# A fused state-space scan and MLP kernel: second x block behind two of five w1 chunks, row-paired matmuls for it, b1 columns from TensorE, first mm2 waiting by w2 chunk, a new order

## The chip, the cores and the metric

One core of a Trainium2 chip runs one launch. The metric is device time in microseconds (us). Every run gives one time; a profiled execution also gives a trace, from which come a page of summaries and answers to single questions. A span in the trace runs from the first to the last instruction and is shorter than the time of the run, which holds what lies around it.

Engines: PE is TensorE (matmuls; its weight loads, LDWEIGHTS, are listed as PEld), DVE is VectorE, ACT is ScalarE, POOL is GpSimd, SP is the sync engine, which here only issues DMAs.

## The reference

x is (1, 2048, 448) in bf16, and the same normalized x feeds two branches:

```
xn  = layernorm(x)
s   = scan(xn)          # complex diagonal state of 448, 2048 steps, plus xn * Dskip
y   = layernorm(xn)
h   = gelu(y @ w1 + b1) # w1: 448 x 1792
g   = silu(h @ w2 + b2) # w2: 1792 x 448
out = x + s * g
```

## The kernel before

**Tiling.** The 2048 rows are taken as 8 blocks of 256, and a block as 128 partitions with two rows each (par 0 and 1, even and odd rows). Four groups g of two blocks (b 0 and 1) pass through the same stages: layernorm statistics on DVE (`ln_stats`, `ln_scale`), application (`ln_apply`), transposition of the normalized rows (`xt`) into `xnT` (scan branch) and `xn2T` (MLP branch), `bu` (PE, L647, the scan's input product), `ssm` (DVE scans, L672), `mm1` (PE, L721, gelu on ACT, L731), `mm2` (PE, L755, bias on DVE L758, silu on ACT L759), and `ym` (PE, L785 to L791, product on DVE L794, addition L797, store).

**The first group is special.** Its MLP input does not come by DMA transposes but by PE: `first_norm` normalizes block 0 in two halves (par 0 and 1; DVE L393, L394, L398; ACT L395, L396), transposes each on PE (L401), copies it out of PSUM on DVE (L405), and five filler matmuls (L403) follow each. Block 1 then gets its statistics on DVE (L379, L383), its scale by ten small DVE instructions (`ln_scale`, L422 to L432), its application (L448), eight transposes on PE (L464) and one copy (L470). `mm1_half(j, b)` computes hidden columns 2j and 2j+1 (two of 14 pieces of 128) for one block: eight matmuls of 128 rows and 256 columns (L741) and one gelu on ACT (L747), seven j for b=0 and then seven for b=1. The bias enters as one more row of w1: `w1_sb[64, 3, :]` holds b1 and the moving operand holds a 1 there.

**mm1 of later groups** has 64-row matmuls. D = 448 is seven times 64, so hidden column 2j+k takes seven passes of 64 rows; passes of the upper and the lower half of the partitions alternate, so that two run at a time. The last 64 rows of w1 must then also lie in partitions 64 to 127: W0 to W3 copy them there (ACT L836 or DVE L837), over the b1 row. The bias comes from `b1f`, columns made from `b1b`, which four small DMAs (B0 to B3) load and POOL casts (BF, L356).

**Loads.** SP issues in order: x block 0 in two halves, x block 1, w1 in chunks (`CH`: 4, 4, 4 and 2 of the 14 pieces; each chunk two DMAs, rows 0 to 383 and the last 64 rows), the scan's B matrices (Bn0, Bn60, Bn1, Bn61), w2 in four chunks, b2, B0 to B3, x blocks 2 and 3, and then the transposing DMAs: two of `xnT` for g=0, seven of `BT` (from the LB results that DVE makes of B), then `xmT1` (`xn2T` of g=1), `Ct` (C matrices), `xnT1`, `xmT0` (`xn2T` of g=2).

**The order.** Every instruction is a numbered or tagged task. `ORDER` is one list of all tasks; an engine takes its own in that order, and waits are semaphores worked out from the keys that tasks read and write. `SECOND` names the tasks that take the second of two possible engines. A task waits once, before its first instruction, for all that it needs: mm2 for all four w2 chunks.

PE's sequence up to g=2 is, in words: 28 warm-up matmuls (L821), the parameter columns (L480 to L484), transposes and fillers of block 0, `mm1_half` j=0 to 4 of block 0, the eight transposes of block 1, j=5 and 6, the seven j of block 1, then mm2, mm2, bu, mm2, bu, mm2, bu (L755 and L647, from 20.01 us on), then mm1 of g=1 (H10 to H16) with two more bu between, and then mm1 of g=2, which begins with H21 at 49.88 us.

Of the kernel before, what the change touches and what calls it, by code (L numbers as in the profile page):

```python
# [7 lines left out]
ACT = mybir.ActivationFunctionType  # L8
ALU = mybir.AluOpType
# [8 lines left out]
class Task:  # L18
# [3 lines left out]
    __slots__ = ("eng", "ins", "reads", "writes", "sem", "idx", "deps", "chain", "alts", "tag")  # L22

    def __init__(self, eng, ins, reads, writes, sem):
# [3 lines left out]
        self.tag = None  # L28
        self.alts = [(eng, ins)]
# [7 lines left out]
class Plan:  # L37
# [55 lines left out]
    def link(self):  # L93
        last, readers = {}, {}
        for t in self.tasks:
            for k in t.reads:
                if k in last:
                    t.deps.add(last[k])
            for k in t.writes:
# [12 lines left out]
    def emit(self):  # L112
# [8 lines left out]
        for t in order:  # L121
# [3 lines left out]
            need = {}  # L125
            for d in t.deps:
                sem, val = done[d]
                if need.get(sem, 0) < val:
                    need[sem] = val
            for sem, val in need.items():  # L130
                if seen.get(sem, 0) < val:
                    eng.wait_ge(self.sems[sem], val)
                    seen[sem] = val
            for k, fn in enumerate(t.ins):
                last = fn(eng)
# [26 lines left out]
0 9 18 22 10 1 19 23 16 20 15 88 2 11 21 3 27 12 26 8 17 14 13 24 5 7 89 25 6 4 28 90 96 91 29 45 97 92 98 30 93 46 94 99 48 49 47 31 103 95  # L162
53 100 50 54 101 32 52 102 55 62 33 105 51 114 56 34 106 35 107 116 108 63 109 64 36 65 DH 37 118 104 38 115 57 39 117 120 66 58 110 119 40
111 122 148 121 41 146 142 143 112 42 123 124 B0 113 147 B1 126 155 60 125 B2 154 61 153 59 149 B3 72 152 128 69 67 44 156 127 68 70 150 151
130 129 160 73 167 132 158 131 168 169 134 159 133 157 136 184 171 135 170 161 138 172 185 173 140 139 175 174 275 43 141 W0 176 186 177 BF
71 137 82 305 74 W1 75 178 187 77 79 179 86 306 76 272 78 304 80 195 81 83 307 310 85 188 309 308 311 276 162 312 189 233 W2 163 281 313 234
316 287 314 322 180 315 317 235 284 W3 164 273 318 323 319 412 278 165 282 192 166 236 410 277 413 190 283 320 285 237 279 196 414 411 193
416 288 H10 238 417 415 280 418 324 181 H11 321 364 366 393 419 H12 422 516 365 183 239 518 368 517 367 191 242 H13 240 522 521 H14 241 182
# [26 lines left out]
def bass_recurrent_scan__ssm_conv_s5__mixer_channel_mlp__prompt_kernel(  # L195
# [18 lines left out]
    with ExitStack() as es:  # L214
# [75 lines left out]
        with nc.Block():  # L290
# [53 lines left out]
            for c in (1, 2, 3):  # L344
                ldw1(c, S1 + 3)
# [568 lines left out]
```

## Time and profile before

| what | value |
|---|---|
| time, median of 3 runs | 156.45 us (156.44 to 156.95) |
| time of the profiled execution | 156.73 us, its span 155.0 us |
| PE busy | 148.7 us, 96% of the span |
| DVE, ACT, POOL busy | 127.2, 108.2, 39.7 us |
| first mm1 matmul (L741) | at 6.74 us |
| first mm2 matmul (L755) | at 20.01 us |
| first mm1 matmul of g=1 (L721) | at 35.46 us |
| first mm1 matmul of g=2 (L721) | at 49.88 us |
| last PE matmul begins its group | at 151.84 us |

How to read the trace's rows: a timeline row gives start, duration, engine, line, operation, tiles and count, and in brackets how long the engine sat idle before it and what ended that. A matmul's duration in the trace holds its way through the array and overlaps the next matmul; the time that one more matmul costs (its pitch) is the difference of the starts. For example 72 matmuls of L741 from 12.15 to 20.01 us have a pitch of 109 ns, though each lasts 273 ns.

### The profile page before, as it was taken

What the parts mean: (1) busy time and instruction counts of PE and PEld (TensorE: products, weight loads), DVE (VectorE), ACT (ScalarE), POOL (GpSimd) and SP (SyncE); (2) the same over time, 40 slices, a digit from 0 to 9 for tenths busy, and PEclk for the clock granted to TensorE, in tenths of its full rate; (3) what the DMA queues carried; (4) which work ended last, traced back from release to release, by engine and by line L of the source; (5) the groups of instructions that cost most, each with busy time, mean ns of one, the idle gap of its engine ahead of it and who ended that gap; (6) DMA issues with size and microseconds to landing.
All of it is one profiled execution on the core that took longest, in us unless ns stands there. A gap on an engine that the chain in (4) does not pass through costs nothing.

```text
span 155.0 us, 3005 instructions
## 1 busy us (share of the span) xinstructions
PE 148.7 (96%) x1072; PEld 90.3 (58%) x1072; DVE 127.2 (82%) x276; ACT 108.2 (70%) x183; POOL 39.7 (26%) x117
## 2 busy tenths in 40 slices
PE   6889999999997999999999999999999999999992
PEld 6789956665553655555544447665666454555551
DVE  5898999989998999889999936369948559984974
ACT  3769899984997799979989793640592893393200
POOL 6575072000036633000049330000471700000021
PEclk9999999999999999999999999999999999999999
DMA  4999999898997003000005340005030000100013
GB/s 118 297 286 353 284 154 185 209 197 195 211 109 153 0 0 68 4 2 0 0 4 127 59 118 0 4 20 98 4 118 0 2 0 0 66 0 0 0 59 118
DMA packets 31512, 14.04 MB, mean 91 GB/s; under 512 B 25733, under 2 KB 31113, under 8 KB 31498
## 3 DMA queue, kind: packets, MB, share of 16 engines
q1 hardware_dynamic: 31344, 13.80, 40.6%
q8 instruction: 8, 0.13, 0.4%
q10 hardware_dynamic: 154, 0.06, 0.1%
q14 instruction: 6, 0.05, 0.1%
HBM read 6.20 MB, written 1.84 MB: 52 GB/s over the span
## 4 chain that ended last, share of the span: by engine, by line
PE 68%; DVE 14%; ACT 7%; DMA 6%; issue 3%; SPq 2%; ACTq 0%; DVEq 0%
PE psum L755 21%; PE psum L721 14%; PE psum L785 13%; PE psum L647 9%; PE psum L788 4%; PE psum L636 4%; DMA w_sb<-in_B_w_dram 3%; DMA xn2T<-xn_sb 2%; ACT WT L579 2%; DVE Bn L598 2%; SPq L90 2%; PE psum L741 2%; DVE lnst L379 2%; DVE xn_sb L448 1%; ACT xn_sb L449 1%
## 5 line engine op out<-in xcount | busy, mean ns | idle before, releaser
L755 PE MATMUL psum<-w_sb,gT 128*128 128x448 bf16 x224 | 44.2, 353 | 0.0
L721 PE MATMUL psum<-xn2T,w_sb 64*128 64x512 bf16 x294 | 33.6, 378 | 1.0 <-DMA xn2T<-xn_sb 0.9
L755 PEld LDWEIGHTS psum<-w_sb,gT 128*128 128x128 bf16 x224 | 21.8, 98 | 19.4 <-issue 0.2
L731 ACT ACTIVATE gT<-psum,b1f 128x512 bf16<-128x512 f32 x42 | 25.7, 687 | 5.2 <-PE psum L721 5.1
L721 PEld LDWEIGHTS psum<-xn2T,w_sb 64*128 64x128 bf16 x294 | 15.9, 109 | 17.1 <-issue 3.0
L647 PE MATMUL psum<-xnT,BT 128*128 128x256 bf16 x196 | 24.0, 273 | 0.0
L647 PEld LDWEIGHTS psum<-xnT,BT 128*128 128x128 bf16 x196 | 18.9, 98 | 5.3 <-issue 0.8
L794 DVE TENSOR_TENSOR t<-psum,g_sb 128x448 bf16<-128x448 f32 (+2 forms) x17 | 10.0, 592 | 9.7 <-PE psum L788 8.8
L759 ACT ACTIVATE g_sb<-o 128x448 bf16<-128x448 f32 x16 | 9.1, 573 | 8.2 <-DVE o L758 8.2
L672 DVE TENSOR_TENSOR_SCAN s_f<-cw,cur,v_sb 128x256 f32<-128x256 f32 x21 | 14.6, 737 | 0.2
L741 PE MATMUL psum<-xn2T,w_sb 128*128 128x256 bf16 x112 | 12.7, 273 | 0.8 <-DVE xn2T L405 0.4
L741 PEld LDWEIGHTS psum<-xn2T,w_sb 128*128 128x128 bf16 x112 | 11.8, 111 | 1.4 <-DMA w_sb<-in_B_w_dram 0.7
L769 POOL TENSOR_TENSOR xr<-xd,g_sb 128x448 f32<-128x448 bf16 x4 | 4.4, 1090 | 31.3 <-ACT g_sb L759 24.3
L758 DVE TENSOR_TENSOR o<-psum,b2bc 128x448 f32<-128x448 f32 x16 | 9.8, 613 | 2.9 <-PE psum L755 2.4
L785 PE MATMUL psum<-CZ,h_sb 128*128 128x448 bf16 x56 | 11.9, 353 | 0.0
L448 DVE TENSOR_SCALAR xn_sb<-x_all,lnw 128x448 bf16<-128x448 bf16 (+1 forms) x31 | 10.8, 382 | 0.9 <-DMA xn2T<-xn_sb 0.7
L651 ACT ACTIVATE u_sb<-psum 128x512 bf16<-128x512 f32 x12 | 7.0, 587 | 5.4 <-PE psum L647 5.4
L785 PE MATMUL psum<-CQ,h_sb 128*128 128x448 bf16 (+2 forms) x54 | 10.5, 332 | 0.0
L747 ACT ACTIVATE gT<-psum 128x512 bf16<-128x512 f32 x14 | 8.3, 595 | 3.1 <-PE psum L741 2.9
L595 ACT ACTIVATE tmp<-Cr,cw 128x448 f32<-128x448 bf16 (+1 forms) x12 | 8.0, 665 | 1.3 <-DVE CQ L598 0.6
L785 PEld LDWEIGHTS psum<-CZ,h_sb 128*128 128x128 bf16 x56 | 5.2, 98 | 5.9 <-issue 0.8
L379 DVE BATCH_NORM_STATS2 lnst<-x_all 128x6 f32<-128x448 bf16 x14 | 8.1, 615 | 0.1
(156 smaller groups left out, 217.4 us busy)
## 6 DMA issues: line engine op xcount, KB each, us to landing
out_dram<-tmp SPq DMA_DIRECT2D x7, 224.0 KB, 1.9
w_sb<-in_B_w_dram SPq DMA_DIRECT2D x3, 448.0 KB, 7.5
x_all<-in_A_x_dram SPq DMA_DIRECT2D x3, 448.0 KB, 4.8
w_sb<-in_B_w_dram SPq DMA_DIRECT2D x3, 384.0 KB, 5.4
Bn<-in_A_B_re_dram SPq DMA_DIRECT2D x1, 336.0 KB, 5.5
Bn<-in_A_B_im_dram SPq DMA_DIRECT2D x1, 336.0 KB, 5.7
x_all<-in_A_x_dram SPq DMA_DIRECT2D x2, 112.0 KB, 2.1
x_all<-in_A_x_dram SPq DMA_DIRECT2D x1, 224.0 KB, 2.8
```

The source lines that it names most:

```text
L379: dve([lambda e, b=b, par=par, q=q: e.bn_stats(lnst[:, q, :], x_all[:, 2 * g + b, par, :])], [f"x{2 * g + b}"] + (["xmT0p1"] if (g, b) == ...
L448: on = [("dve", [lambda e, o=o, i=i: e.tensor_scalar(o, i, rs, nb, op0=ALU.mult, op1=ALU.add) for o, i in pairs], 0.4, 0.12), ("act", [lam ...
L647: fns = [lambda e, r=r, m=m, d=d: e.matmul(psum[:, 4, r * NK:(r + 1) * NK], BT[:, m, d, :], xnT[:, gx, d, :], start=(d == 0), stop=(d == 6 ...
L672: dve(lambda e, i=i, ri=ri, init=init: e.tensor_tensor_scan(s_f[:, i, ri, :], col(R2, i).to_broadcast([128, NK]), v_sb[:, i, ri, :], init, ...
L721: return lambda e: e.matmul(psum[:, b0 + k, :], w1_sb[halves[h], d, fcol(2 * j + k)], rhs[halves[h], d, :, :], start=first and d == 0, sto ...
L731: act([lambda e, k=k: e.activation(gT[:, gb, 2 * j + k, :], psum[:, b0 + k, :], ACT.Gelu_apprx_tanh, bias=b1f[:, 2 * j + k:2 * j + k + 1]) ...
L741: fns = [lambda e, k=k, d=d: e.matmul(psum[:, banks[k], :].rearrange("p (r c) -> p r c", r=2)[:, :, cs], w1_sb[:, d, fcol(2 * j + k)], rhs ...
L755: fns = [lambda e, fi=fi: e.matmul(psum[:, bk, 0:D], gT[:, gb, fi, q * 128:(q + 1) * 128], w2_sb[:, fi, :], start=(fi == 0), stop=(fi == N ...
L758: dve(lambda e: e.tensor_tensor(o2[:, ob, :], psum[:, bk, 0:D], b2bc[:], ALU.add), [f"ps{bk}", "b2bc"], [f"oo{ob}"], 0.62, prio - 76)
L759: act(lambda e: e.activation(g_sb[:, gs, :], o2[:, ob, :], ACT.Silu), [f"oo{ob}"] + (["silu"] if g == 0 else []), [f"g{gs}"], 0.58, prio - ...
L785: fns = [lambda e, k=k: e.matmul(psum[:, bk, c0:c1], h_sb[:, hb, k, k0:k0 + 128], cm[:, k, c0:c1], start=(k == 0), stop=False) for k in ra ...
L794: dve(lambda e: e.tensor_tensor(t3[:, fb, c0:c1], psum[:, bk, c0:c1], g_sb[:, gs, c0:c1], ALU.mult), [f"ps{bk}", f"g{gs}"], [f"t3{fb}_{c0} ...
```

## The change

Parts, in words:

1. `CH` has five chunks (4, 4, 2, 2, 2) and SP issues chunks 0 and 1 of w1 before x block 1; the fifth chunk's two DMAs are w4 and r4. w2 comes in pieces of 4, 4, 2 and 4; Bn60 and Bn61 are issued behind w2.
2. `b1b`, its four DMAs and the cast on POOL go. PB, 14 matmuls of one row, makes the b1 columns from the b1 row of w1, and AB copies them to `b1f` on ACT.
3. Block 0's first two j are taken per half: Q0 and Q1 (par 0), then tasks 114 and 116 (par 1), eight matmuls of 128 columns each.
4. Block 1 gets its scale on POOL in pieces (`second_norm`: R0, R1, and task 109), its application and transposes per half (tasks 110, 111 on DVE; 112 and T1 on PE, five transposes each; 113 and K1 on DVE). The transposes write the last 64 rows to both halves of the partitions, and block 1's mm1 (`mm1_second`, G0 to G6) has the 64-row form, with the bias from `b1f` and two gelus for each j. W0 to W4 now all run on DVE, ahead of it.
5. mm2 of g=0 waits for w2 chunk by chunk (`late`).
6. The 28 warm-up matmuls of 128 columns become seven of 512; POOL's `sine` chain is split in two (SA); `ORDER` and `SECOND` are new.

```diff
+            for k, fn in enumerate(t.ins):
+                need = {}
+                for d in t.ldeps.get(k, ()) if k else t.deps:
...
-            CH = ((0, 4), (4, 4), (8, 4), (12, 2))
+            CH = ((0, 4), (4, 4), (8, 2), (10, 2), (12, 2))
...
-            for c, (a, n) in enumerate(CH):
-                kb.tag = f"B{c}"
-                ld("sp", b1b[:, a:a + n], dram_ap(B_b1, a * 128, [[n, 128], [1, n]]), [f"b1b{c}"], 256 * n, S1 + 6)
-            kb.tag = "BF"
-            pool(lambda e: e.tensor_copy(b1f[:], b1b[:]), [f"b1b{c}" for c in range(4)], ["b1f"], 0.3, S1 + 6)
+            ld("sp", w2_sb[:, 10:14, :].rearrange("p (c n) d -> p c (n d)", c=2), dram_ap(B_w2, 1280 * D, [[2 * D, 128], [256 * D, 2], [1, 2 * D]]), ["w2_3"], 392000, S1 + 6, dur=0.9)
...
+                kb.tag = "PB"
+                pe([lambda e, fi=fi: e.matmul(psum[:, 4, fi:fi + 1], w1_sb[64:65, 3, fcol(fi)], ident[64:65, 64:65], start=True, stop=True) for fi in range(NF)],
+                   W1B + ["ident"], ["ps4"], 0.4, 3 * PINNED)
+                kb.tag = "AB"
+                act(lambda e: e.activation(b1f[:], psum[:, 4, 0:NF], ACT.Copy), ["ps4"], ["b1f"], 0.2, 3 * PINNED)
...
+            def second_norm():
+                half = lambda n: mhalf[:, 0, 0:1].to_broadcast([128, n])
+                for par in range(2):
+                    q = 2 * par + 1
+                    w, r1, var = lnw[:, 0, 0, 1, q:q + 1], lnw[:, 0, 2, 1, q:q + 1], lnmv[:, 0, q, 1:2]
+                    kb.tag = f"R{par}"
+                    kb.add("pool", [lambda e, w=w, var=var: e.tensor_scalar(w, var, 1.0 + LN_EPS, LN_EPS * LN_EPS, op0=ALU.mult, op1=ALU.add),
+                                    lambda e, w=w, r1=r1: e.tensor_tensor(r1, w, mhalf[:, 0, 0:1], ALU.pow)], [f"mv0_{q}", "mhalf"], [f"r1b{par}"], dur=0.7, lat=0.15, chain=True)
...
+            def mm1_first(j, prio):
...
+                rows = [slice(r, r + 1) for r in range(2)] if j < 2 else [slice(0, 2)]
+                for r in rows:
+                    if j < 2 and r.start == 0:
+                        kb.tag = f"Q{j}"
+                    pe([lambda e, k=k, d=d, r=r: e.matmul(psum[:, b0 + k, :].rearrange("p (r c) -> p r c", r=2)[:, r, 0:128], w1_sb[:, d, fcol(2 * j + k)],
+                                                          rhs[:, d, r, :], start=(d == 0), stop=(d == 3)) for k in range(2) for d in range(4)],
...
+            def mm1_second(j, prio):
...
+                def half(k, d, h):
+                    first = h == k
+                    return lambda e: e.matmul(psum[:, b0 + k, :].rearrange("p (r c) -> p r c", r=2)[:, :, 128:256], w1_sb[halves[h], d, fcol(2 * j + k)],
+                                              rhs[halves[h], d, :, :], start=first and d == 0, stop=not first and d == 2)
+                kb.tag = f"G{j}"
+                pe([half(k, d, k) for d in range(4) for k in range(2)], rd, banks, 0.43, prio)
+                pe([half(k, d, 1 - k) for d in range(3) for k in (1, 0)], rd, banks, 0.33, prio)
...
+                if g == 0:
+                    kb.tasks[-1].late = {4: ["w2_1"], 8: ["w2_2"], 10: ["w2_3"]}
```

What the new `ORDER` says for each engine up to g=2, decoded from its numbers:

```
PE   warm-up, parameter columns, PB, block 0 transposes and fillers, Q0 Q1 114 116, j=2 3 4 5,
     112 T1, j=6, G0 to G4 (own and other parts), mm2, G6 G5, mm2, mm2, bu, mm2, bu,
     H10 H11 H12 H13 with bu, H15 with bu, H14 H16, bu, H21 H20
DVE  copies of block 0, four ra (L564) and L566, W0, statistics of block 1, W1, 110 111, W2, 113,
     W3, K1, W4, three L568, LB3 LB0 (L598), LB4 LB1, mm2 bias, statistics and scale of g=1,
     xm1 (L448), mm2 bias, xm0, mm2 bias, LB2, LB5, statistics of g=2, LB6, scale and xm of g=2
POOL ..., wrap, SA, R0, R1, rest of sine, 109, the parameter chain
ACT  ..., r11, cp, cdt, dcol, AB, r0, cr, gelus of block 0, two gelus for each j of block 1, tables
SP   x0 x0 w1_0 w1r_0 w1_1 w1r_1 x1 w1_2 w1_3 w1_4 Bn0 Bn1 w2 (four) Bn60 Bn61 b2 x2-3 Dskip,
     xnT0_0 BT0 Cs0 BT3 xnT0_1 x4-5 BT4 BT1 xmT1_1 xmT1_0 x6-7 BT2 BT5 Ct2 BT6 Ct1 xnT1_1 Ct3
     xnT1_0 Ct0 xmT0_0 Cs1 xmT0_1
```

At the end, PE's last five tasks are `ym` of the last group. Before they are 599, 596, 603, 607, 611, so that the last is a seven-matmul part of 192 columns; in the change they are 596, 599, 607, 611, 603, so that the last is the eleven-matmul part of 448 columns (112 KB of output instead of 48 KB).

## The prediction

> **What bounds the kernel now.** I read the page's busy shares first, then what TensorE (PE) waited for, then its timeline at the start, then the chain that ended last near PE's longest wait, then SP's queue there.
>
> ```profile
> span 155.0 us, 3005 instructions
> ...
> PE 148.7 (96%) x1072; PEld 90.3 (58%) x1072; DVE 127.2 (82%) x276; ACT 108.2 (70%) x183; POOL 39.7 (26%) x117
> ```
>
> PE is the bound: 155.0 - 148.7 = 6.3 us is all that it does not work, start and tail included.
>
> ```profile
> PE psum L821 <- POOL mhalf L314: 1.4, 1, 1.4
> PE psum L721 <- DMA xn2T<-xn_sb: 0.9, 1, 0.9
> PE psum L741 <- DVE xn2T L405: 0.4, 1, 0.4
> PE psum L741 <- DMA w_sb<-in_B_w_dram: 0.4, 1, 0.4
> ```
>
> PE's waits (total, times, longest). Besides the start there are three: 0.4 for block 0's copies, 0.4 for w1's second chunk, 0.9 for a transposing DMA.
>
> ```profile
> 4.62 0.25 PE L484 MATMUL psum<-ident,vrows 4*128 4x4 bf16 x4
> 4.95 0.40 PE L401 MATMUL psum<-ident,xn_sb 128*128 128x128 bf16 x4
> ...
> 6.74 1.91 PE L741 MATMUL psum<-xn2T,w_sb 128*128 128x256 bf16 x16 [0.44 <-DVE xn2T L405]
> 9.05 2.81 PE L741 MATMUL psum<-xn2T,w_sb 128*128 128x256 bf16 x24 [0.41 <-DMA w_sb<-in_B_w_dram]
> 11.70 0.61 PE L464 MATMUL psum<-ident,xn_sb 128*128 128x128 bf16 x8
> 12.15 8.02 PE L741 MATMUL psum<-xn2T,w_sb 128*128 128x256 bf16 x72
> ```
>
> Pitches: L741 costs (20.01 - 12.15)/72 = 109 ns, the transposes L464 (12.15 - 11.70)/8 = 56 ns, tiny matmuls (L480 to L484, nine from 4.34 to about 4.84) 56 ns.
>
> ```profile
> 45.89 0.41 DVE pa L667
> 46.31 3.44 DMA xn2T<-xn_sb
> 49.75 0.14 issue
> 49.88 3.21 PE psum L721 x28
> ```
>
> The chain (start, us, what): PE's longest wait, for H21, ends when the second transposing DMA of g=2 lands, 3.44 us after its issue. SP, which issued it, had been full:
>
> ```profile
> 30.27 2.75 SPq L89 DMA_TRANSPOSE xn2T<-xn_sb  x2
> 33.06 1.31 SPq L89 DMA_TRANSPOSE Cr<-in_A_C_im_dram  x1
> 34.47 1.24 SPq L89 DMA_TRANSPOSE BT<-Bn  x1
> ...
> 39.61 1.23 SPq L89 DMA_TRANSPOSE xnT<-xn_sb  x1
> 40.88 3.43 SPq L89 DMA_TRANSPOSE Cr<-in_A_C_re_dram  x2
> 44.35 0.58 SPq L90 DMA_DIRECT2D h_sb<-in_A_C_im_dram  x1
> 45.03 2.61 SPq L89 DMA_TRANSPOSE xn2T<-xn_sb  x2
> ```
>
> A transposing DMA holds SP for 1.2 to 1.4 us and there is nearly no gap from 30.27 to 47.6. After 49.88 PE never waits again until its last matmul (timeline, 49.88 to 151.5: 101.6 of 101.6 us busy). And the work that PE does before H21 is the same set of tasks in both orders. So **all of the front is worth only what it moves H21**; then come the new order and the tail.
>
> **Part by part, up to H21.** *PB* adds 14 tiny matmuls at 56 ns: 0.78 us, behind the parameter columns (end 4.84) and ahead of block 0's first transposes, which went at 4.95. These go at 5.6, so +0.67. Their copies (0.54 after L401's start before) then end near 6.55 and 6.97, and Q0, which needs only the first, starts near 6.8, against 6.74. Waiting for one half hides what PB costs. PB also waits for the b1 row, a 3.5 KB DMA issued at 2.23 on ACT's queue; the trace gives no landing, the vector rows issued until 2.19 on that queue had landed by 4.34. Bounds 4.3 and 6.7 (nobody needed it before L741); I take 4.6. Behind PB on PE stands block 0 itself, and AB holds ACT's r0 and cr by some 0.6, which end at 6.6; the gelu table load (1.28) still ends at 7.9, before the first gelu.
>
> *Halved j=0, 1*: 32 matmuls of 128 columns for 16 of 256 (1.75). Nearest row L464, 56 ns: 1.8 us; upper bound the 109 of L741: 3.5. Weights read with a stride load in 113 ns there against 98, so I take 56 x 113/98 = 65: 2.1, +0.3. The end is 8.9. [...]
>
> *w1_1 ahead of x1*: 224 KB less ahead at 285 to 297 GB/s (the slices there) is 0.8, so it lands near 8.3, and PE's 0.41 wait goes. j=2 starts at 8.9 (9.05 before). *x1* later, near 9: DVE first does ra, L566 and W0 until 9.5 (from L564 1.5, L566 0.69, L837 0.33), so that is hidden. *Transposes* 10 for 8: +0.1. *Block 1 in 64 rows*: 98 matmuls of 256 columns. L721 with 512 columns keeps 28 in 3.15, or 112 ns each, 225 a pair. Half the columns: at best 56 (no pitch in this trace is lower), 14 x 56 = 0.78 for a j; at worst weight loads (109) one after another, 1.53. Two loads already overlap in L721 (294 of 109 ns in 15.9 us), so I take 0.81 against 8 x 109 = 0.87: -0.4 in seven.
>
> *Block 1's chain*: DVE, from rows: statistics until 11.0, W1 and 110 until 12.1, 111 until 12.5, 113, W3, K1 until 13.9. PE reaches 112 at 12.35, T1 at 12.9, G0 at about 14.1: 0.2 of waiting. R0 and R1 stand behind SA (five of about 0.32, from 9.3 on, when ACT's Abs is done) on POOL: R0 from 10.9. Each has a power; the one such row is L424, 1.72 us for 8 columns. For one column the bounds are 0.39 (L695, 128x1) and 1.72; I take 0.4, the row nearest in shape. Behind them POOL holds the rest of sine and the parameter chain for LB.
>
> Sum at the first mm2: 6.8 + 2.1 + 4.35 (five j) + 0.56 + 0.2 + 4.05 (G0 to G4) = 18.1, and with G5 and G6 (1.6) 19.7 against 20.01: -0.3. *Late w2 waits*: the last w2 DMA was issued at 10.8 and landed 8.2 later, 19.0; the tenth matmul comes at 18.1 + 10 x 0.19 = 20.0, no wait; at worst 1. Then four mm2 (2.65) and two bu (1.53): H10 at 33.4 instead of 35.46 (one bu moves behind it), and with 14.9 us more (H10 to H16 at 1.575, bu 1.53, 0.77, 1.53) PE is **ready for H21 at 48.4**.
>
> Is its input? DVE and SP: the first mm2 ends at 20.8; bias 0.6, statistics 2.7, scale 2.0, xm1 with xd 1.6 gives 27.9; xm0 29.7, LB2 31.4. SP: xmT1_1 28.1, xmT1_0 29.8, x6-7 31.2, BT2 31.8, and BT2 and the ten issues behind it take 13.1 us by the rows if Ct1 and Ct0 are 1.2 each (as Ct2, Ct3), 14.1 if 1.7 each, and up to 0.5 of gaps: xmT0_1 is issued between 44.9 and 46.4 and lands 3.5 later, so **the data come between 48.4 and 49.9**. BT2 and BT5 have moved into this queue, Cs0 out. I take 49.3, nearer the upper end, as Ct1 and Ct0 are the very issues that took 1.7: **-0.6** at H21, most of PE's gain turning into a wait of 0.9, as now.
>
> DVE loses ten small instructions (2.0) and gains W1 to W4 (0.9), ACT loses W1 to W3 (1.7) and gains seven split gelus (7 x (2 x 0.38 - 0.60) = 1.1): not on the path. Warm-up: 7 x 427 by 28 x 107 ns, the same 3.0.
>
> **Tail.** The last part is 448 wide: product 0.60 and addition 0.38 for 0.35 and 0.44, landing 1.7 for 1.6, SP's issue instead of ACT's: +0.25. **Sum**: -0.6 + 0.25 = -0.35. The profiled 156.73 becomes 156.4; that run lies 0.28 over the median of 156.45, so against the median: **156.1**.
>
> **The rivals.** *Transposes in time* (0.27): if SP gets its inputs a us earlier, H21 starts at 48.4, -1.5, +0.25: 155.2. For it: g=2's normalization is one block on DVE now, where before it was split around the scans. Against: the SP rows above. *POOL late* (0.12), the slower side: if a power costs 1.72, R1 ends near 14.9 instead of 12.3; T1, K1 and G0 follow, G0 at 16.2, first mm2 and with it DVE's statistics and SP's chain 2 us later: 156.1 + 2 = 158.1. It decides once R1 ends after 12.6. For it: L422 on POOL took 0.82 at 45.03, beside DVE's L666, and L426 0.26 elsewhere. [...] *A new wait behind H21* (0.09): the orders differ there throughout; one late transposing DMA costs 0.9 (as now) to 3.4: 157.5. *64-row halves or PB do not do what they say* (0.06): 7 x (1.53 - 0.81) = 5, less the 0.9 of wait at H21: 160.
>
> **How the numbers follow.** My forecast has 0.46; its own range is 155.3 to 156.9. About 0.5% (0.8 us) is what a measurement can tell: faster means below 155.7, slower above 157.2. Forecast: 0.09 faster, 0.32 same, 0.05 slower; with the rivals faster 0.36, same 0.32, slower 0.32. The range 154.8 to 158.0 leaves out the last rival, the upper half of the two before, and a little below.
>
> **What would show it.** PE's wait before H21 near 0.9 us on the xn2T DMA, with H21 at 49 to 50; no wait on w1 near 9; G0 near 14; 14 L721-like matmuls of 256 columns in about 0.8; R1's end near 12.3. Wrong, if H21 starts by 48.5, if PE waits after it, or if the power takes over 1 us.

## The result and the profile after

| | before | changed |
|---|---|---|
| time, median | 156.63 us (156.44 to 156.95) | 161.76 us (161.04 to 162.96) |
| ratio | 1 | 1.0333, 95% interval 1.0267 to 1.0399 |
| profiled execution, its span | 156.73, 155.0 us | 162.96, 161.2 us |
| H21 starts | 49.88 | 53.86 |
| H21 to the last matmul | 101.96 | 103.72 |
| last matmul to the end of the span | 3.16 | 3.57 |

The change made the kernel 5.1 us slower, where 0.35 us faster was forecast. Of the 6.2 us between the two profiled spans 4.0 lie in front of H21, 1.8 behind it and 0.4 in the tail. The profiled execution of the changed kernel is the slowest of its four; the others have spans of 159.2 to 160.2, so a single pair of profiles shows about 1 us more than the medians. Ratios are of fast runs, and where single executions of a version below were slow (two of four with Abs and 109 moved and PB late, one of four with the scale on DVE) its time is the median of the others.

First the chain that ended last, shares of the span by engine, before:

```profile
PE 68%; DVE 14%; ACT 7%; DMA 6%; issue 3%; SPq 2%; ACTq 0%; DVEq 0%
```

and after:

```profile
PE 45%; ACT 17%; DVE 15%; DMA 8%; POOL 6%; issue 5%; SPq 1%; ACTq 0%; DVEq 0%
```

PE's busy share is as it was (152.9 us, 95%), but its share of the chain fell by 23 points, and 18 of them went to ACT, POOL and DMA: the order is no longer one that PE alone sets. The changed kernel's PE timeline (start, duration, what, and in brackets the idle time before it and what ended it):

```profile
5.37 0.58 PE L412 MATMUL psum<-ident,w_sb 1*128 1x1 bf16 x14 [0.29 <-DMA w_sb<-in_B_b_dram]
7.36 6.93 PE L772 MATMUL psum<-xn2T,w_sb 128*128 128x128 bf16 x64
14.85 0.52 PE L879 MATMUL psum<-ident,xn_sb 128*128 128x128 bf16 x5 [0.22 <-DVE xn_sb L439]
16.28 4.56 PE L789 MATMUL psum<-xn2T,w_sb 64*128 64x256 bf16 x70
20.78 1.50 PE L804 MATMUL psum<-w_sb,gT 128*128 128x448 bf16 x7
...
53.86 3.21 PE L748 MATMUL psum<-xn2T,w_sb 64*128 64x512 bf16 x28 [1.75 <-ACT gT L758]
```

PB waits for the b1 row (5.37). Q0 begins at 7.36, and its 64 matmuls (32 of 128 columns, 32 of 256) take 6.77 to the next line's group: by the starts of the single matmuls the 128-column ones went at 107 ns each until 10.45 and at 56 ns after that, 3.27 us for 32. G0 is at 16.28 and the first mm2 at 20.78, and H21 waits 1.75, for ACT.

Now POOL's timeline after:

```profile
10.95 0.24 POOL L528 TENSOR_SCALAR ang<-ang 128x16 f32<-128x16 f32 x1 [2.44 <-ACT ang L537]
...
12.78 0.67 POOL L430 TENSOR_TENSOR lnw<-lnw,mhalf 128x1 f32<-128x1 f32 x1
...
13.80 0.56 POOL L430 TENSOR_TENSOR lnw<-lnw,mhalf 128x1 f32<-128x1 f32 x1
...
16.22 0.97 POOL L433 TENSOR_TENSOR lnw<-lnw,mhalf 128x2 f32<-128x2 f32 x1
...
17.83 0.40 POOL L546 TENSOR_TENSOR cw<-cw 128x4 f32<-128x4 f32 x1
18.18 0.35 POOL L546 TENSOR_TENSOR cw<-cw,ang 128x4 f32<-128x4 f32 x2
```

and the row that answers to the last of these before:

```profile
12.29 0.20 POOL L519 TENSOR_TENSOR cw<-cw,ang 128x4 f32<-128x4 f32 x1
```

The parameters that need the sine come at 18.2 instead of 12.3. Ahead of them POOL waited 2.44 for ACT's Abs (L537), which stands behind block 0's first gelu, and it ran R0, R1 (0.67 and 0.56 for a power of one column) and 109 (0.97 for two columns). What waits for POOL, on DVE:

```profile
10.84 0.29 DVE L897 COPY w_sb<-w_sb 64x512 bf16<-64x512 bf16 x1 [1.18 <-PE psum L772]
11.16 0.63 DVE L384 BATCH_NORM_STATS2 lnst<-x_all 128x6 f32<-128x448 bf16 x1
...
19.31 0.18 DVE L560 RECIPROCAL cw<-cw 128x4 f32<-128x4 f32 x1 [1.15 <-POOL cw L549]
19.50 0.82 DVE L623 TENSOR_SCALAR tmp<-Bn,cw 128x448 f32<-128x448 bf16 x2
```

The rows that answer to these before, and SP's first transposing DMA of BT (BT0):

```profile
6.58 1.15 DVE L379 BATCH_NORM_STATS2 lnst<-x_all 128x6 f32<-128x448 bf16 x2
9.91 0.17 DVE L533 RECIPROCAL cw<-cw 128x4 f32<-128x4 f32 x1
15.39 0.45 DVE L596 TENSOR_SCALAR tmp<-Bn,cw 128x448 f32<-128x448 bf16 x1
20.13 2.57 SPq L89 DMA_TRANSPOSE BT<-Bn  x2
```

Block 1's statistics stand behind the copy W0 (L897), which overwrites the b1 row and so waits for PE's halved j: they begin at 11.16 (6.58 before). The reciprocal was at 9.91 before and is at 19.31 now, with the first products of B (LB) behind it. Most of these 9.4 us were slack: before, the first product stood behind other work of DVE and began at 15.39, so it is 4.1 later now (19.50). Its result lets BT0 go 1.6 later, and SP's queue is:

```profile
14.94 2.34 SPq L90 DMA_TRANSPOSE xnT<-xn_sb  x1
21.73 1.22 SPq L90 DMA_TRANSPOSE BT<-Bn  x1
...
39.13 2.83 SPq L90 DMA_TRANSPOSE BT<-Bn  x1
...
47.33 1.28 SPq L90 DMA_TRANSPOSE Cr<-in_A_C_re_dram  x1
48.66 1.31 SPq L90 DMA_TRANSPOSE xn2T<-xn_sb  x1
50.01 0.58 SPq L91 DMA_DIRECT2D h_sb<-in_A_C_im_dram  x1
50.68 1.23 SPq L90 DMA_TRANSPOSE xn2T<-xn_sb  x1
```

SP stands still from 17.3 to 21.7 (waiting for LB) and is then full until 52: the second transposing DMA for H21 goes at 50.68, 4.4 later than before (46.31). It stretches by 2.8 from BT0 to there: one transposing DMA more (the second xnT of g=0, 1.3, which went ahead of BT0 before), and waits for LB (BT6's issue at 39.13 took 2.83 and not 1.24). ACT stands behind the same queue:

```profile
47.33 3.43 DMA Cr<-in_A_C_re_dram
50.76 0.03 ACTq L138
50.79 0.05 issue
50.83 0.67 ACT tmp L622
51.50 0.67 ACT gT L758 x2
```

This is the chain of waits in front of H21. The combine at 50.83 (task 197) waits 2.93 for Ct0 with the gelus of g=1 behind it, and H21 needs PSUM banks that those gelus read. H21's own input was no earlier: the DMA issued at 50.68 landed 3.0 later, at 53.7, and H21 began at 53.86. Taking ACT's wait alone away would have moved H21 by no more than 0.2.

### The profile page after: what moved, and what is told of

Read it like the earlier page. It is cut to its first block, busy times and chain, and to the rows that moved or that the text cites. A ratio compares the mean times of both kernels' runs of the same rounds, so it can differ in the third digit from the quotient of the medians.

```text
span 161.2 us, 3085 instructions
## 1 busy us (share of the span) xinstructions
PE 152.9 (95%) x1117; PEld 88.0 (55%) x1117; DVE 126.1 (78%) x266; ACT 109.6 (68%) x192; POOL 45.7 (28%) x125
## 4 chain that ended last, share of the span: by engine, by line
PE 45%; ACT 17%; DVE 15%; DMA 8%; POOL 6%; issue 5%; SPq 1%; ACTq 0%; DVEq 0%
PE psum L836 12%; PE psum L748 11%; PE psum L674 8%; PE psum L804 7%; DMA BT<-Bn 4%; PE psum L839 4%; ACT xn_sb L474 3%; ACT tmp L622 3%; ACT gT L758 3%; DVE CQ L625 2%; DMA Cr<-in_A_C_re_dram 2%; DVE s_f L699 2%; PE psum L772 2%; DMA w_sb<-in_B_b_dram 2%; ACT gT L795 2%
## 5 line engine op out<-in xcount | busy, mean ns | idle before, releaser
L804 PEld LDWEIGHTS psum<-w_sb,gT 128*128 128x128 bf16 x224 | 21.7, 98 | 19.4 <-issue 0.4
L748 PEld LDWEIGHTS psum<-xn2T,w_sb 64*128 64x128 bf16 x294 | 15.2, 104 | 18.4 <-ACT gT L758 2.5
L699 DVE TENSOR_TENSOR_SCAN s_f<-cw,cur,v_sb 128x256 f32<-128x256 f32 x21 | 15.5, 773 | 0.1
L820 POOL TENSOR_TENSOR xr<-xd,g_sb 128x448 f32<-128x448 bf16 x5 | 6.1, 1225 | 29.4 <-ACT g_sb L810 17.4
L474 ACT ACTIVATE xn_sb<-x_all,lnw 128x448 bf16<-128x448 bf16 (+1 forms) x18 | 11.8, 682 | 2.6 <-POOL lnw L454 1.8
L703 ACT ACTIVATE s_b<-s_f 128x1536 bf16<-128x1536 f32 x4 | 5.9, 1479 | 10.6 <-DVE s_f L699 10.5
L820 POOL TENSOR_TENSOR xr<-x_all,xr 128x448 f32<-128x448 bf16 x5 | 6.0, 1194 | 19.3 <-DVE xr L821 19.3
L836 PE MATMUL psum<-CQ,h_sb 128*128 128x448 bf16 (+2 forms) x54 | 10.6, 332 | 0.0
L622 ACT ACTIVATE tmp<-Cr,cw 128x448 f32<-128x448 bf16 (+1 forms) x8 | 5.3, 666 | 4.8 <-DMA Cr<-in_A_C_re_dram 2.9
L473 DVE TENSOR_SCALAR xn_sb<-x_all,lnw 128x448 bf16<-128x448 bf16 (+1 forms) x22 | 7.0, 354 | 1.6 <-DMA xnT<-xn_sb 1.3
```

What stands on the lines that cost most here:

```text
L474: ("act", [lambda e, o=o, i=i: e.activation(o, i, ACT.Identity, bias=nb, scale=rs) for o, i in pairs], 0.75, 0.2)]
L622: on = [("act", [lambda e, o=o, i=i, c=c: e.activation(tmp[o, k, :], b[i], ACT.Copy, scale=c[i]) for o, i, c in ps], 0.66 * len(ps), 0.2), ...
L699: dve(lambda e, i=i, ri=ri, init=init: e.tensor_tensor_scan(s_f[:, i, ri, :], col(R2, i).to_broadcast([128, NK]), v_sb[:, i, ri, :], init, ...
L748: return lambda e: e.matmul(psum[:, b0 + k, :], w1_sb[halves[h], d, fcol(2 * j + k)], rhs[halves[h], d, :, :], start=first and d == 0, sto ...
L804: fns = [lambda e, fi=fi: e.matmul(psum[:, bk, 0:D], gT[:, gb, fi, q * 128:(q + 1) * 128], w2_sb[:, fi, :], start=(fi == 0), stop=(fi == N ...
L820: kb.either(("pool", lambda e, o=o, i0=i0, i1=i1, op=op: e.tensor_tensor(o, i0, i1, op), 1.37, 0.15), ("dve", lambda e, o=o, i0=i0, i1=i1, ...
```

## The experiments

All ran beside the kernel before, on the same chip, whose median was 156.4 to 156.95. "Pitch halves" means the time at which 128-column matmuls go from 107 to 56 ns each. H21 and the distance (from H21 to the start of the last matmul) are those of the profiled execution.

### The slow start of TensorE

After with the warm-up of before, and before with that of after:

```diff
 (the changed kernel)
-[... to_broadcast([128, 4, 128]) ... for _ in range(7)]
+[lambda e: e.matmul(psum[:, 3, 0:128], ident[:, :], ident[:, :], ...) for _ in range(28)]
 (the kernel before, the other way round)
-[lambda e: e.matmul(psum[:, 3, 0:128], ident[:, :], ident[:, :], ...) for _ in range(28)]
+[... to_broadcast([128, 4, 128]) ... for _ in range(7)]
```

> The changed kernel with the warm-up of before: 28 matmuls of 128 columns, each with its own weights, in place of 7 of 512. Both take about 3.0 us. T1 (the shape of the warm-up keeps TensorE slow): the tiny matmuls and block 0 run at 56 ns from about 4.1 us, the 32 halved matmuls take 1.8 to 2.1 us and not 3.27, the first gelu starts near 8.5 and not 10.2, G0 near 14.5 to 15, H21 at 50.5 to 52.5 and not 53.9; time 158.0 to 160.0. T2 (what keeps it slow is the gap behind the warm-up, the waits at 4.40 and 5.09 with the PB matmuls, whatever the shape): TensorE stays at 107 ns until about 10.4 us, the time stays at 161 to 162.

161.29 us, ratio 1.027 (1.0207 to 1.0334). The pitch halves at 9.27, not at 4.1; H21 at 52.73.

> The kernel before with the warm-up of after, 7 matmuls of 512 columns, and nothing else changed. T1: the tiny matmuls and block 0's transposes run at 107 ns, the full pitch comes about 3 us after block 0 has begun to keep TensorE busy (near 9 to 10 us instead of 4.06), the first gelu starts 1 to 2 us later; H21 moves by 0 to 2 us as the slack of 0.9 us there allows; time 157 to 159. T2: the gap behind the warm-up is short here (the next matmuls wait for the vector rows alone), so the pitch is 56 ns from about 4.5 us and the time is 156.4 to 156.9.

156.65 us, ratio 0.9993 (0.9951 to 1.0036). The transposes of block 0 still go at 107, L741 from 7.15 at 108 for 256 columns, so the clock is up by then. **The form of the warm-up explains neither the clock nor the time.**

A longer one:

```diff
-... for _ in range(7)]
+... for _ in range(9)]
```

> The changed kernel with a warm-up of 9 matmuls of 512 columns instead of 7: it ends 0.85 us later, at 5.25. In the traces so far TensorE's pitch halved at 4.1, 5.1, about 7, 9.2, 9.2 and 10.4 us, with either form of the warm-up. [...]

161.64 us, ratio 1.0323 (1.0262 to 1.0384). The pitch halves at 10.45 and Q0 begins at 7.67 (10.45 and 7.36 in the changed kernel): the longer warm-up brought no earlier rise.

PB moved out of the way:

```diff
-97 92 PB 98 30 ... 47 31 AB 103 ... 56 116 153 115 152 r4 118
+97 92 98 30 ... 47 31 103 ... 56 116 PB 153 115 152 r4 AB 118
```

> The changed kernel with the 14 b1 matmuls (PB) moved behind block 1's first matmuls of the statistics on TensorE, and their copy (AB) behind the gelus there, so that nothing stands between the parameter columns and block 0. T2 (the gap and PB keep the clock low): TensorE is at 56 ns by 4.5 to 7 us and the first half of the gain of a fast front comes back: 158 to 160. T1: TensorE is still at 107 ns until some 3 us after block 0 begins, but block 0 begins up to 1.0 us earlier (no wait of 0.29 on b1 and no 14 tiny matmuls of 53 to 107 ns): Q0 near 6.4 and not 7.4, the time 160 to 161.5. The first gelu needs AB only if its bias does; then it comes later and eats this.

160.78 us, ratio 1.0249 (1.0177 to 1.032). Here TensorE was at full pitch from 5.1, and the front went much as forecast (lines are one higher in this kernel):

```profile
6.01 1.95 PE L773 MATMUL psum<-xn2T,w_sb 128*128 128x128 bf16 x32
7.89 0.57 PE L413 MATMUL psum<-ident,w_sb 1*128 1x1 bf16 x14
8.78 3.66 PE L773 MATMUL psum<-xn2T,w_sb 128*128 128x256 bf16 x32 [0.32 <-ACT b1f L416]
...
13.85 1.05 PE L773 MATMUL psum<-xn2T,w_sb 128*128 128x256 bf16 x8
14.83 4.56 PE L790 MATMUL psum<-xn2T,w_sb 64*128 64x256 bf16 x70
19.33 2.82 PE L805 MATMUL psum<-w_sb,gT 128*128 128x448 bf16 x14
```

32 halves in 1.88 (2.1 estimated), and yet H21 only at 51.60, after 1.4 us of waiting for the transposing DMA. **PB's place goes with the rise in 17 of 20 profiles.** The kept traces record when the granted clock changed, and the rise falls where the pitch halves (4.09 before, 10.46 in the changed kernel, 5.10 here). With the PB matmuls (one row, one column each) ahead of block 0 it rose at 8.87 to 10.53 in seven of eight profiled executions (4.92 in the eighth); without them by 6.80 in ten of twelve (7.39 and 9.82 in the others), whichever warm-up there was.

Other things differ between the kernels too. In the changed kernel PE waited 0.29 for the b1 row and then ran PB from 5.37 to 5.89; the clock rose at 10.46. The longer warm-up has PB and no such wait, and its pitch halved at 10.45. Late PB with 109 and M moved and the scale on DVE has no PB there and a wait of 0.3 (L406), and the clock rose at 9.82. The kernel before has the parameter columns alone, and it rose at 4.09. In late PB it rose at 5.10, with 109 and M moved as well at 7.39: what else sets the moment is not shown.

By this pair of profiles a fast start is worth 2.3 of the 4.0 at H21, with the 14 PB matmuls among it, and 1.7 are left with it. Another pair with the same two fronts (53.37 and 52.13, "Behind H21") gives 1.2. In the medians it is 1.0, and the intervals overlap.

### What holds SP, and what POOL does

ACT's Abs (task 57) ahead of the first gelu:

```diff
-116 153 115 152 r4 118 156 34 57 117 SA
+116 153 57 115 152 r4 118 156 34 117 SA
```

> The changed kernel with one step moved in the order: ACT's Abs for the sine goes ahead of block 0's first gelu. TensorE's slow start stays. POOL waited 2.44 us for this Abs; the Abs then starts near 9 us and not 10.65, R1 ends near 13.2 and not 14.4, the parameter chain reaches DVE's reciprocal some 1.2 us earlier. If the parameter chain is what makes SP late, H21 starts 0.5 to 1.5 us earlier, 52.4 to 53.4, and the time is 160 to 161; if H21 hangs on ACT's order alone (task 197, which waits for a late DMA and has the gelus of G0 behind it), H21 moves by less than 0.3 and so does the time (161 to 162).

161.23 us, ratio 1.0262 (1.0197 to 1.0328); H21 at 52.78, BT0 at 21.25. Nothing that the time could tell from the changed kernel. The Abs began at 9.46 and not 10.65, but the load of the gelu's table (1.28), which was over at 8.0 in the changed kernel, now comes behind it, and the first gelu begins at 10.98 and not 10.16.

The same with 109 behind the parameters, in the changed kernel and with late PB:

```diff
-K1 109 42 ... 131 61 132
+K1 42 ... 131 61 109 132
```

> The changed kernel with two steps moved: ACT's Abs ahead of block 0's first gelu, and on POOL the four instructions of block 1's second scale (109, with a two-column power of 0.97) behind the seven parameter instructions that the first product of B waits for. Theory P (the front of POOL's queue is the late step: Abs, the powers of R0 and R1 and 109 stand ahead of the parameters, these reach DVE's reciprocal at 19.3 instead of 9.9, BT0 leaves SP at 21.7 instead of 20.1, and SP is full from there to H21 and to the loads of C): the reciprocal runs near 16 to 16.5, BT0 is issued near 18.5 to 19.5, the transposing DMAs for H21 1.5 to 2.5 us earlier, H21 at 51.0 to 52, time 158.8 to 160. Rival (SP waits for ACT's other block 1 instead, or DVE is what is full behind 20 us): BT0 early, but H21 within 0.5 of 53 and the time above 160.5.

160.43 us, ratio 1.0263 (1.0191 to 1.0335); BT0 at 19.79, H21 at 51.65. This is the profile in which the clock rose at 4.92.

> The same two steps in the version with late PB. Theory P: BT0 near 18.5 instead of 20.26, both inputs of H21 by 50.2, so H21 at 50.2 to 50.5 without a wait, and the loads of C early as well, so that the gain is not handed to the C products as it was when Ct0 was only put behind: last matmul near 153.8, time 159.0 to 159.8. Rival: as in that run, H21 moves and TensorE waits as much behind it: 160.4 or more.

162.42 us (161.53 and 163.31), ratio 1.0374 (1.0271 to 1.0476); H21 at 54.86. Neither tells the theories apart, by my own edit: the Abs waits for POOL, and with it ahead, the table load, ACT's gelus and AB wait as well. The longest PE waits at L772 of the two, in the view of waits (us in total, times, longest):

```profile
PE psum L772 <- ACT gT L775: 1.9, 1, 1.9
```

```profile
PE psum L772 <- ACT b1f L415: 3.1, 1, 3.1
```

So 109 was moved alone, the Abs where it was:

> The changed kernel with one step moved: 109 (the second scale of block 1, four instructions on POOL with a power of 0.97) behind the seven parameter instructions, and the Abs where it was. Theory P (POOL's powers ahead of the parameters are what makes BT0 and SP late): the reciprocal 1.9 us earlier than in the changed kernel (17.4 if TensorE starts as slow, 16 if fast), BT0 near 19.8, H21 1.0 to 1.9 earlier, at 52 to 52.8; time 159.9 to 160.8. Rival (SP's queue alone): BT0 earlier, but H21 by less than 0.5 and the time 161.2 or more.

161.03 us (159.5 to 161.1), ratio 1.0273 (1.0209 to 1.0338): H21 came a little earlier than the 52 to 52.8 of theory P, the time did not come down to its 159.9 to 160.8. TensorE started as slowly as in the changed kernel (pitch halves at 10.6), the reciprocal came at 18.32 and not 19.31, BT0 at 20.60, and PE:

```profile
51.94 1.27 PE L748 MATMUL psum<-xn2T,w_sb 64*128 64x512 bf16 x10 [0.28 <-ACT gT L758]
```

**H21 is 1.9 earlier than in the changed kernel for one moved step of four POOL instructions**, and its wait is 0.28 and not 1.75. Two other profiles with 109 in its old place and a start as slow (H21 at 53.37 and 53.20) make it 1.4 and 1.3. In the medians it is 0.6 (4.6 over the kernel before, and not 5.1); these intervals overlap, so this rests on the traces. What is left is PE's: with this wait gone, it is ready no earlier than 51.7.

The opposite: block 1's scale back on DVE, ten small instructions in place of R0, R1 and 109.

```diff
-                    kb.add("pool", [... ALU.pow)], [f"mv0_{q}", "mhalf"], [f"r1b{par}"], dur=0.7, lat=0.15, chain=True)
...
+                kb.add("dve", fns, ["mv0_1", "mv0_3"], ["r1b0", "r1b1", "lnw0_1"], dur=2.05, lat=0.12, chain=True)
```

> The changed kernel with block 1's scale on DVE as before the change (ten small instructions, about 2.05 us, for the three steps R0, R1 and 109 on POOL). POOL is free of 3.7 us, DVE has 2.05 more ahead of xm1. Theory P: the parameters reach the reciprocal near 15.5 to 16 instead of 19.3, BT0 near 18, H21 1.5 to 2.5 earlier, at 51.4 to 52.4, though block 1's transposes may come up to 0.7 later; time 159.2 to 160.3. Rival (DVE and SP are what is full): the 2.05 on DVE come back as a later block 1 and later products of B, H21 at 53 or later, time 161.5 to 163.

162.70 us, ratio 1.0428 (1.0345 to 1.051). The rival held (H21 at 53.30): PE waited for block 1,

```profile
15.26 0.97 PE L878 MATMUL psum<-ident,xn_sb 128*128 128x128 bf16 x10 [1.71 <-DVE xn_sb L438]
```

and the reciprocal came at 18.83, now because DVE itself was late. This interval overlaps that of the changed kernel, so that POOL is the better place for this scale in this order rests on the last run of "Behind H21", where the intervals are apart; its fault is the place in POOL's queue, ahead of the parameters.

### SP's queue, and where a wait goes

Late PB with Ct0 (183), Cs1 (182) behind H21's DMAs and their users later:

```diff
-251 424 H16 197 250 372 248 199 376 ... H21 375 252 200
+251 424 183 182 H16 250 372 248 376 ... H21 375 197 252 199 200
```

> The late-PB version with two of SP's DMAs moved: Ct0 (the transposing load of C) and Cs1 go behind the two transposing DMAs that H21 reads, and the combines that need Ct0 go on ACT behind the gelus of g=1 and on DVE behind the scans. In the late-PB version's trace those DMAs were issued at 46.36 and 48.39, H21 came at 51.60 after 1.4 us of waiting, and TensorE was ready at 50.2. Theory S (SP's full queue sets H21): both are issued 1.3 to 1.9 us earlier, H21 comes at 50.2 to 50.5 without a wait, and the time falls by 1.0 to 1.4 against 160.8, to 159.4 to 159.8. Rival (ACT's late gelus set it as well, or the combines now late hold TensorE behind H21): H21 moves by under 0.5, or it moves and TensorE waits as much behind it; time 160.5 to 161.5.

160.67 us, ratio 1.0267 (1.0202 to 1.0332), the last matmul at 154.99 as in late PB alone (155.01). H21 moved to 50.27 without a wait, just as theory S had it, and PE then waits at the C products:

```profile
50.27 3.21 PE L748 MATMUL psum<-xn2T,w_sb 64*128 64x512 bf16 x28
...
61.47 1.50 PE L663 MATMUL psum<-CQ,Bn 128*128 128x448 bf16 x7 [1.06 <-DVE CQ L625]
```

Both H21 and the C products hang on the same SP queue, and here what one gained the other lost. The edit also moved two combines back, so it does not show whether the late DMA or the late combines made the C products late. The same in the kernel before, with Ct1 (191), Cs1 and five combines moved back and g=2's scaling (423, 420) forward:

```diff
-517 367 191 242 ... H14 241 182 370 369 423 519 372 424 420 371 ... 421 373
+517 367 242 ... H14 423 420 241 370 369 519 372 424 371 ... 421 191 182 373
-248 197 H15 ... 326 198 376 ... 374 201 377 ... H20 199 202 375
+248 H15 ... 326 376 ... 374 377 ... H20 375 197 198 201 199 202
```

> The kernel before with SP's Ct1 and Cs1 behind the two transposing DMAs that H21 reads, g=2's scaling on DVE ahead of one product of the scan, and the five combines that need Ct1 behind the gelus of g=1. In the trace of before H21 waited 0.9 us for the second of these DMAs, issued at 46.31. Theory S: they are issued near 43 and 44.3, H21 starts when TensorE is ready, at 49.0, and the time falls by 0.5 to 0.9 to 155.5 to 155.9. Rival: the combines come late and TensorE waits behind H21 for the C products, so that the time stays or rises to 157.

160.11 us, ratio 1.0196 (1.0138 to 1.0254), slower than the rival's 157: H21 came at 48.94 without a wait, the C products (L636) waited 2.5, and after that pause the matmuls ran at half the rate for 3.2 us (below).

### Behind H21

The old order from H21 on, after the changed front, and after the front with late PB:

```diff
-H21 375 252 200 H20 ... 604 605 606
+H21 (the remaining tasks as in the order of before)
```

> The changed kernel with everything behind H21 in the order of the kernel before (and the choices of ACT or DVE that belonged to it); up to H21 nothing is changed. From H21 to the last matmul the traces show 101.96 us before and 103.4 to 103.8 in four kernels with the new order, and from there to the end 3.16 against 3.57. Theory N (the new order behind H21 costs 1.5 to 1.9, its tail 0.4): H21 stays at 52.5 to 54, the distance falls to 102.0 to 102.4 and the tail to 3.2, time 159.5 to 160. Rival (the distance is what a late H21 leaves behind, since DVE and SP come late into it): the distance stays at 103.3 or more, time 161 to 162.

165.29 us, ratio 1.0514 (1.0437 to 1.0591); H21 at 53.37, distance 107.7.

> Late PB and the old order behind H21 together. If the two are independent, their gains add: H21 at 51.6, 102.0 to 102.4 behind it, tail 3.2: a span of about 157, time 158.5 to 159.2. If the distance behind H21 is only what a late H21 leaves behind, time 160 to 161.

163.92 us, ratio 1.046 (1.0385 to 1.0535); H21 at 52.13, distance 108.1. **The old order does not bring the old distance back.** It does its C combines where DVE, after this front, is not ready for them:

```profile
67.48 2.06 PE L663 MATMUL psum<-CQ,Bn 128*128 128x448 bf16 x7 [2.90 <-DVE CQ L625]
```

(the first of the two). An order fits the front that it was made for, so these two runs do not show what the new order costs behind a front that fits it. What is left behind H21 are short waits. One move aims at those for M: g=3's scaling on ACT (525, 528), which waits for a power of 2.27 on POOL, behind the copy of M (214), in the version with late PB and the Abs early:

```diff
-268 331 525 269 387 220 528 526 223 527 214 270
+268 331 269 387 220 223 214 525 528 526 527 270
```

> The version before this one (late PB, POOL's steps moved), with g=3's scaling on ACT behind the second copy of the C product (M). In the traces of the new order ACT stood idle for 2.36 us at 64.7, waiting for POOL's power of g=3 (2.26 us), with that copy behind it, and TensorE lost 0.37 at 69.1 and 0.28 at 73.5. Theory N (such queues of the new order are what costs 1.5 behind H21): these two waits go, the distance from H21 to the last matmul falls from 103.4 to about 102.9, time 0.4 to 0.7 below the version before this one. Rival: the transposing DMAs of g=3, now later, or the next copy take their place; no change or up to 0.5 slower.

162.29 us, ratio 1.0366 (1.0289 to 1.0443), beside 162.42 and 1.0374 for the version without it: no difference in time. In the profiles the wait at M (0.29) is gone, one at the C products grew from 0.16 to 0.36, and the distance is 103.47 and not 103.89. These two share the 3 us that AB lost in front.

All at once: late PB, 109 behind the parameters, M's copy free.

> Late PB, 109 behind the parameters, and g=3's scaling on ACT behind the second copy of M; the Abs where it was. In late PB alone TensorE was ready for H21 at 50.2 and waited 1.4, BT0 went at 20.26. Theory P: BT0 at 18.4 to 18.9, H21 at 50.2 to 50.5, behind it 102.8 to 103.0 (the two waits at M gone), tail 3.57: span 156.5 to 157.0, time 158.3 to 158.8. Rival: H21 at 51.3 or later, or the wait returns at the C products; 159.8 or more.

159.66 us, ratio 1.0205 (1.0155 to 1.0255), apart from the changed kernel's interval: 1.9 of the 5.1 us are explained and taken back, less than theory P had expected (158.3 to 158.8). H21 at 50.71, 0.8 after the kernel before and 3.2 ahead of the changed kernel; distance 103.59, tail 3.63. Of the 3.2 us that are left this profile shows 0.8 in front of H21, 1.6 behind it and 0.5 in the tail; no run takes these back. Its PE waits from H21 on:

```profile
PE psum L748 <- ACT gT L758: 0.3, 1, 0.3
PE psum L674 <- DMA xnT<-xn_sb: 0.2, 1, 0.2
PE psum L836 <- DVE h_sb L731: 0.2, 1, 0.2
PE psum L663 <- DVE CQ L625: 0.2, 1, 0.2
PE psum L836 <- DVE o L809: 0.2, 1, 0.2
```

M is gone from the list, and DVE's combines and scans have come in.

The same with the scale on DVE:

> As the run before this, with block 1's scale on DVE instead of POOL. Theory P: H21 at 50.0 to 50.5 as there, since TensorE is what is last then, unless block 1's transposes wait longer for DVE (0.9 in late PB); time 158.2 to 159.0. Rival: DVE's 2.05 delay xm1 and with it all of TensorE by 0.7 or more; 159.2 to 160.

162.33 us, ratio 1.0359 (1.0291 to 1.0426), H21 at 54.46: as above, PE waits for block 1 (1.22). Part of the 3.7 us at H21 is the clock, which rose at 9.82 in this profile and at 7.39 in the one before.

### One part alone, and a better kernel

The kernel before with Cs1 behind H21's DMAs, and that with the first two chunks of w1 (four DMAs) ahead of the second x block as well:

```diff
-H14 241 182 370 ... 524 421 373
+H14 241 370 ... 524 421 182 373
 (and, in the second)
-27 12 26 8 17 ... 91 29 45
+27 12 8 17 ... 91 29 26 45
```

> The kernel before with one DMA moved: Cs1 (0.58 us of SP) behind the two transposing DMAs that H21 reads. Its user, the transposing load of Ct4, goes some 1.2 us later and is read at 54.4 in the trace. Theory S: the second of H21's DMAs is issued 0.6 earlier (45.7 instead of 46.31), H21 comes at 49.3 instead of 49.88, and nothing behind it gets a new wait: 0.4 to 0.6 below the kernel before, a ratio near 0.997. Rival (DVE gives the data no earlier, or the combines of C wait for Ct4): ratio 0.999 to 1.003.

155.97 us, ratio 0.9957 (0.9923 to 0.999): 0.4% below the kernel before, just clear of 1, and the lowest median of all that ran. PE has no wait at H21 (48.46, 1.4 earlier in the profiled execution; 0.6 is the issue taken out, and the rest was there already at BT0, 19.70 instead of 20.13, and in the issues up to it).

> The same with the change's step at the front: w1's second chunk issued ahead of the second x block. TensorE's wait of 0.41 us for that chunk goes, Q, the first mm2 and TensorE's readiness for H21 come 0.4 earlier; x's second block lands 0.8 later, while DVE's statistics of it began at about 6 in the kernel before. If TensorE's front is worth something, H21 comes at 48.9 to 49.3 and the ratio is 0.994 to 0.997; if SP and DVE set H21 whatever TensorE does in front (as my prediction said of the change), it is as the run before this one, or slower by what DVE loses, 0.997 to 1.003.

157.52 us, ratio 1.0047 (1.0018 to 1.0076): against the run before it, the change's own first step costs 1.5 us here, and the ratio lies above the 0.994 to 1.003 expected. DVE and PE of this run:

```profile
8.66 1.15 DVE L379 BATCH_NORM_STATS2 lnst<-x_all 128x6 f32<-128x448 bf16 x2 [2.21 <-DMA x_all<-in_A_x_dram]
```

```profile
12.99 0.62 PE L464 MATMUL psum<-ident,xn_sb 128*128 128x128 bf16 x8 [1.54 <-DVE xn_sb L448]
```

PE has no wait at w1 (nor had the run beside it; the kernel before had 0.41) and loses 1.54 at block 1: DVE begins on x's second block 1.8 to 2.1 later (6.82 in the run beside it, 6.58 in the kernel before), not the 0.8 expected. Those 0.8 were the bytes of the block itself (224 KB), which w1 no longer waits for; what the block now waits for are four DMAs of w1 with 896 KB. SP takes 2.21 to issue them, so the block is issued at 3.97 and not 1.71, and it lands 4.7 after its issue and not 2.8.

## Why the prediction was wrong

| step | forecast | changed | late PB (fast start) |
|---|---|---|---|
| Q0 | 6.8 | 7.36 | 6.01 |
| 32 halves | 2.1 | 3.27 | 1.88 |
| block 1's statistics end | 11.0 | 12.73 | 10.88 |
| R1 ends | 12.3 | 14.36 | 12.84 |
| G0 | 14.1 | 16.28 | 14.83 |
| one j in 64 rows | 0.81 | 0.90, later 0.82 | 0.90, later 0.82 |
| first mm2 | 18.1 | 20.78 | 19.33 |
| PE ready for H21 | 48.4 | 52.1 | 50.2 |
| second xmT0 issued | 44.9 to 46.4 | 50.68 | 48.39 |
| H21 | 49.3 | 53.86 | 51.60 |

H21 was to come when PE was ready for it (48.4) and its input was there (48.4 to 49.9). Both failed: PE was ready 3.7 later, and input and banks came 1.75 after that.

- **The step that failed on the input's side: "Behind them POOL holds the rest of sine and the parameter chain for LB."** This sentence had no price, and it is the chain that makes BT0, and so all of SP, late. The forecast came to SP's BT2 (31.8; it was 34.64, and 33.39 with a fast start) from the first mm2 through DVE, with no term for the parameters, LB and BT0, and gave the rest 13.1 to 14.1 us; it took 16.0 (15.0 with a fast start), through waits for LB. 109 alone is worth 1.3 to 1.9 at H21, though in the run that moved it the first mm2 was no earlier (21.02).
- **The step that failed on PE's side: "Warm-up: ... the same 3.0", with PB priced as time alone.** The duration was right, and PB with its wait took 0.81 for the 0.78 forecast. What was put at nothing is the clock: with PB and its wait of 0.29 ahead of block 0 it rose at 10.46, with PB late at 5.10. The changed kernel, whose halves ran at 107 ns until 10.45, lost 1.4 in them (3.27 and not 1.88), and more through W0, which holds block 1's statistics until PE has done them, and through the Abs behind the first gelu. By late PB this and PB's own 0.9 cost 1.2 to 2.3 at H21. That the form of the warm-up was the cause was my first theory, and it fell.
- With both steps mended PE was ready at 50.4 and H21 came at 50.71, 3.2 earlier than in the changed kernel.
- **The powers**: the forecast took 0.4 for one column, from a row (L695) that is no power but the mean of three multiplications (0.19, 0.19 and 0.79); they took 0.67 and 0.56, and 0.97 for two. R1 ended after 12.6, the point from which the rival "POOL late" was to decide, but its mechanism was another: a power of 1.72, G0 at 16.2, and from there the first mm2, DVE and SP. G0 came at 16.28 by luck, as R1 ended late mostly because the statistics ended 1.7 late, and the way that counted on POOL went through LB.
- **x1 "hidden"**: in the changed order it is, as DVE has other work first. But that order pays for it with statistics at 9.3 to 11.2 instead of 6.6, and where that is not rearranged the step costs 1.5.
- **64-row halves**: the form did what was forecast, 108 ns for a pair, and five of the seven groups of 14 matmuls took 0.76 to 0.86 (0.81 forecast). But in all 15 traces with this form the third and the fifth group took 1.02 to 1.10, in the changed kernel with a stop of 0.33 in the weight loads behind matmuls of the same line. So the seven took 6.13, as much as in 128 rows (6.10), and the gain of 0.4 was not there. Why the loads stop stays open.
- **The late w2 waits** cost nothing, as said; the first mm2 had no wait. **w1_1**: its 0.41 went, as said. The tail: +0.41 for +0.25. (The sum for PE's readiness adds up to 48.3, not 48.4.)
- **"A new wait behind H21"** (forecast as a rival of 0.09, at 1.4) came beside the others: the distance is 1.2 to 1.9 longer in every kernel with this order, apart from the one where a wait at the C products came in, made of waits at M, the C products and the scans: in the changed kernel six of them put off the next matmul by 0.2 to 0.4 each, 1.8 in all, where the kernel before has none. In 12 to 20 us DVE was busy 5.92 (7.54 before) and ACT 5.40 (7.25): that this work, put off while all waited for POOL, is what comes late behind H21 is argued from these numbers, not shown.

The rule that all of the front is worth only what it moves H21 was right, and incomplete: the C products are a second such point, with 0.3 to spare in the kernel before (last CQ at 59.6, read at 59.87), as the runs with Ct and its combines moved show.

## What to carry to other kernels

When a step moves to another engine, price what stands behind it in that engine's queue, not only who waits for its result: four small POOL instructions here held DVE's reciprocal, SP's queue and ACT's gelus in turn. SP's queue, full here from 21.73 to 51.91, passed a delay of its first entry on (BT0 1.6 later, H21's second DMA 4.4 later, 2.8 of it added on the way), so look for the last reader of each entry, and be ready for a relieved wait to come up at the next one. When a load moves behind others, count the bytes and the issues that now go ahead of it, not its own; look who is idle for it. And when tiny matmuls or a wait go right behind a short warm-up, look when the pitch halves: with PB there it did so at 10.45 in the changed kernel, where PE showed as busy (2.00 of 2.00 us from 8 to 10), and with PB late at 5.10.

## What was not expected of the hardware

**Around a pause of 2.51 us the clock halved.** Where PE waited 2.51 (the kernel before with Ct1 moved, L636 at 61.61), seven matmuls of 448 columns then took 2.57 to the next line's, 367 ns each, where the seven at 66.07 took 1.33, 190 each, and full rate came back 3.2 us later; the granted clock by stretches of 1 us (PE, PEld, DVE, ACT and POOL busy, then PEclk):

```profile
61.00:62.00 1.00, 0.39 (x2) 0.20 (x3) 1.00 (x4) 1.00 (x2) 0.92 (x3) 0.70 2.21 145
62.00:63.00 1.00, 1.00 (x4) 0.40 (x3) 1.00 (x3) 1.00 (x3) 0.02 (x1) 0.50 0.16 29
63.00:64.00 1.00, 1.00 (x4) 0.46 (x3) 1.00 (x3) 0.07 (x1) 0.00 (x0) 0.50 0.48 105
64.00:65.00 1.00, 1.00 (x8) 0.67 (x6) 1.00 (x3) 0.47 (x1) 0.00 (x0) 0.59 0.00 0
65.00:66.00 1.00, 1.00 (x12) 0.90 (x10) 1.00 (x3) 0.98 (x2) 0.00 (x0) 1.00 0.00 0
```

Four more profiles with pauses of 2.82 to 3.10 have it as well (mean granted clock 0.987 to 0.989), those with pauses of 1.4 to 1.9 do not (0.997 to 1.000). The same kernel can escape it: of its four runs three had a mean granted clock of 0.989 and 160.01 to 160.41 us, the fourth 1.000 and 158.97; why is not shown. At the start of the kernel the same column reads 1.00 (4 to 10 us in the changed kernel) while single matmuls take 107 ns instead of 56, since the record of the clock begins with its first rise: there it has to be read from the starts of the matmuls.

A power on POOL took 0.56 and 0.67 us for one column and 0.97 for two (changed kernel), 0.87 for two with 109 behind the parameters, and for eight 1.72 (before) and 2.26 (changed), where the multiplication and addition beside it (L429) took 0.19.
